# Chunk attention and a token-mixing MLP in one kernel: five units' exponentials taken from PSUM with a bias, and another order of steps and loads

## The chip, the cores and the metric

The kernel runs on one core of a Trainium2 chip. The metric is the device time of one execution in microseconds (us); a time without a unit is in us. Engines: TensorE (PE; its weight loads are PEld), VectorE (DVE), ScalarE (ACT), GpSimd (POOL) and SyncE (SP). POOL, SP and ACT can issue DMAs.

## The reference

Two stages, joined. Attention within chunks of 64 tokens (8 batches, 8 heads, 576 tokens, head size 64):

```python
scores = scale * np.matmul(q_c, k_c.transpose(0, 1, 2, 4, 3))
scores = scores - np.max(scores, axis=-1, keepdims=True)
attn = np.exp(scores)
attn = attn / (np.sum(attn, axis=-1, keepdims=True) + 1e-09)
out = np.matmul(attn, v_c)
```

Its output, with the heads side by side (x: 8 x 576 x 512), goes through the mixer, `relu((x wq)(x wk)^T x * scale) @ w_out`, with wq and wk of 512 x 64 and w_out of 512 x 512. The output is float32, 8 x 576 x 512; inside the kernel the operands of the matmuls are float16.

## The kernel before, in words

**Units.** The work is cut into 20 units, in the order of the list `pairs`. Of each batch, two units hold 256 tokens each (four chunks; "wide"), and the last 64 tokens of two batches make one unit of 128 tokens ("rest"). So units 0 and 1 are batch 0, unit 2 is the rest of batches 0 and 1, units 3 and 4 are batch 1, and so on; 2, 7, 12 and 17 are rests.

**Steps of a unit**, by the names that the code gives them:

- `tq`: PE transposes q, then k, into PSUM (L387, for a rest L372). `qkt`: ACT or DVE copy q's two halves into a block-diagonal tile `qbd` (64 partitions each; called qt below) and k into `kt` (L308, the helper `copy`).
- `S`: the scores into two PSUM banks (L407; a rest takes one). `mx`: DVE takes the maximum of every row (L420). `sub`: DVE subtracts it from the scores, out of PSUM into the SBUF tile `sh`; for wide units it also puts the tokens, which the loads interleave in twos, in their own order (L431, for a rest L427). `exp`: one ACTIVATE on ACT turns `sh` (128x1024 or 128x512) into the float16 tile `es` (L441).
- `E`: PE transposes `es` (L453); `et`: a copy out of PSUM. `V`: PE multiplies by v, with a column of ones that gives the sum (L484), in two halves for a wide unit. `den`, `rec`, `x`: DVE divides into `xs` (L498, L502, L512).
- `xT`, `xt`, `pj`, `wt`, `wkT`, `wkn`: the mixer's transposes, projections and copies (L536, L553, L569). `G`: the product of a batch (L607), copied as `g16`; `clr` clears a part of a `g16` tile beforehand. `mix`, `rm`: the product with g and the relu (L647; L667 on DVE, L669 on ACT). `out`: the last product (L696); `osb`: its copy out of PSUM, in two parts for a wide unit; then the store.

**The order.** Nothing is scheduled at run time. The steps are numbered as they are made, and the string `ORDER` lists the numbers with a letter for the engine: `p` PE, `a` ACT, `v` DVE, then PSUM banks; `206a` is exp of unit 7 on ACT, `207p4` its E in bank 4, `182` et of unit 6, `183` its first V. `i7.256` is a filler: a matmul of ones into bank 7 that nobody reads (L740); there are 52. `592s` sends the store of step 592. Each engine runs its own share of this list in its order, and waits at each instruction for what that instruction needs. The costs written beside the steps (`vec`, `act`, `quart`) served to make the order; they do nothing at run time.

**Loads.** The first unit's q and k come as float32 on SP's queue (L207) and are cast. All others go out on POOL's queue, cast to float16 on the way, in the order of `LOADS`: `q5` is q, then k of unit 5 (L215; L212 for a rest), `v3` its v in two DMAs (L229, L222), `wqk` and `wo` the weights (L233, L236). In the built program each DMA on this queue waits for the one eight before it. Loads are issued as early as `load_more` lets them: a v whose buffer is reused only after its user's V is in the list. Seven buffers serve q and k.

**Stores** go out on SP's queue. Until unit 4's v has been asked for they are kept in a list (`held`), and SP waits for that load with a tiny DMA (L268); the stores are at L271 and L275.

Of the kernel before, what the change touches and what calls it, by code (L numbers as in the profile page):

```python
# [29 lines left out]
class Banks:  # L30
# [8 lines left out]
HELD = 4  # L39
# [8 lines left out]
    "mx1": 2,  # L48
    "sh2": 2,
# [17 lines left out]
LOADS = "q1 v0 q2 v1 wqk v2 q3 q4 v3 q5 wo v4 q6 v5 q7 v6 q8 v7 q9 v8 q10 v9 q11 v10 q12 v11 q13 v12 q14 v13 q15 v14 q16 v15 q17 v16 q18 v17 q19 v18 v19"  # L67
# [5 lines left out]
0a 1v i7.256 i6.256 i5.256 i7.256 i6.256 i5.256 i7.256 i6.256 i5.256 i7.256 i6.256 i5.256 i7.256 i6.256 i5.256  # L73
i7.256 i6.256 i5.512 i7.256 i6.256 7p0 3a 2a 9a 8v i7.512 i6.512 i5.512 i7.512 i6.512 i5.512 i7.512 i6.256
i5.256 10p1 11a i7.256 26p5 28a 4a 27a i7.256 12p0 29p4 13v 30a 14v 15a i7.512 i6.512 i3.512 i7.512 i6.256 31p4
32v i7.512 i6.512 i3.512 i7.256 53p0 55v 33v i7.512 i6.256 16p1 54a 56a 17a 34a i7.512 i6.512 i3.512 i7.512
i6.256 18p0 22p6 i5.256 57p4 i3.512 35p5 36a 23v 19v 20v 58v 24v 59v 21v 37p2 41p4 38v 60a 39v 42v 25v 61p0
88p1 62a 63p6 89a 90a 45p0 40v 64v 43v 65v 44v 91p2 66v i3.256 47p1 92a 67p3 93p6 107p2 i5.512 110p4 109a 108a
68a 46a 48v 6v 94v 5v 95v 111v i3.256 69p5 49p3 70v 71p2 72v 112p4 113v 96a 50a 97p6 51p7 98a 52v 153p3 156p6
73p7.2 103p0 154a 155a 157a 75a 74a 114v 99p4 104v 105v 100v 101v 106v 102v 115a 158p2 76p6 159v 77a 78p0 116p4  # L80
126p5 79a 117v 160v 118p6 122p0 84p4 172p2 175p3 123v 124v 119v 125v 173v 174v 120v 85v 121v 161a 127a 162p5
176a 163a 177p2 168p4 164p0 128p6 129a 199p6 130p7 178v 165v 166v 179v 169v 167v 82p2 131v 170v 200a 202a 201a
180a 203p6 132p7 204v 83a 171v 181p3 234p2 133a 182a 134p7.0 183p4 237p3 236a 136a 235a 135v 205v 184v 185v
186v 238a 137p0 239p2 139p6 206a 138a 207p4 86p5 208a 140a 253p4 240v 241v 256p0 209p6 187p2 255a 254a 242a
143p1 191p4 192a 257v 188v 189v 190v 210v 211v 258p2 212v 259v 145p0 146a 260v 193p4 243p6 194a 244a 87a 87s
299p0 302p4 249p6 245p2 300a 301a 144v 213p5 214a 195p1 196a 261a 250v 251v 246v 303v 252v 247v 248v 215p0
304p4 80p6 149p2 216a 217p7 197p0 150a 198a 305v 218v 318p1 306v 219p0.7 321p2 221v 322v 220a 319a 320a 222p4
272p7 223v 224p2 273a 323p0 262p7 324v 225a 263a 307a 147p4 226p5 345p7 325v 268p0 264p2 148a 148s 81v 81s 269v
265v 270v 266v 271v 227v 267v 308p4 230p6 346a 348a 347a 326a 309a 231a 349p7 380p0 310p4 314p2 383p6 350v 351v
315v 311v 312v 316v 382a 381a 352a 274p1 327p7 328a 151p0 275a 384v 385p6 313v 317v 386v 276p1 353p2 277a 152a  # L90
152s 354a 387v 228p3 229v 229s 337p1 278p0 338a 279a 333p4 329p6 334v 330v 335v 331v 332v 336v 399p2 280p3.0
402p1 355p6 282v 356v 357v 358v 401a 281a 400a 388a 232p3 339p0 340a 283p4 284v 359p2 285p6 341p0 403a 360a
342a 233a 233s 286v 404p4 361p2 389p1 343p0 295p6 362a 363p2 344a 364a 390a 296a 405v 406v 445p3 365p2.0 448p1
366v 367a 447a 395p6 449v 289p0 141p2 370p4 293p1 142a 142s 407a 294a 290a 396v 397v 398v 446v 371v 450p2 451v
408p6 368p4 297p7 409a 369a 298a 298s 467p6 464p0 466a 465a 452v 468v 414p2 410p4 391p6 392v 411v 415v 393v
394v 412v 416v 413v 417v 291p1 376p0 469p6 470v 374p4 453a 454p5 375a 471v 455a 420p2 418p4 421a 419a 377a
491p5 456p2 460p6 287p4 472a 493v 494v 457v 492v 461v 462v 463v 495p5 458v 496v 497v 459v 422p0 378p6 423a 288a
288s 424p0 473p7 425a 529p4 426p0.5 474v 498a 379a 379s 530a 475p6 428v 479p2 427a 476v 480v 526p4 292a 292s
477v 481v 478v 545p0 527a 528a 482v 429p6 499p1 430v 431p2 531p4 500a 432a 485p1 532v 548p6 501p2 502v 439p7
547a 549a 546a 503v 504v 533v 483p6 440a 484a 486a 534a 505p0 550p2 372p7 441p4 487p1 535p6 373a 373s 442a 551v  # L100
506v 552v 437p7 507p0 536a 553a 537p2 488v 508v 541p4 538v 509p6 489p0 542v 539v 554p1 510a 543v 540v 544v 490a
555a 511p0.6 560p2 556p4 561v 557v 562v 558v 559v 563v 438a 438s 512a 513a 564p7 516p0 435p6 514p4 566p2 443p3
515v 565a 517a 567a 568p2 433p7 569a 444a 444s 570p2 436a 434a 434s 571v 522p4 572p6.5 524p7 525a 574v 573v
523v 523s 577p2 575p0 578a 518p7 520p6 576v 519a 521a 521s 589p0 581p7 583p6 585p2 579p3 590a 584a 584s 586a
586s 587p2 591p6 580v 592v 588v 582a 582s 592s 588s
# [4 lines left out]
def kernel(  # L110
# [10 lines left out]
    nc = tc.nc  # L121
# [74 lines left out]
    def load_qk(u):  # L196
        b, m = pairs[u]
        if m is None:
# [4 lines left out]
        for t, x in enumerate((q, k)):  # L203
            if u == 0:
                rows = x[b, :, 0 : 2 * P, :].rearrange("h (p r) d -> p h (r d)", r=R)
                wide_in.append(home("osb", [P, 2, DM], F32))
                nc.sync.dma_start(wide_in[t][:].rearrange("p i (h e) -> p (i h) e", e=R * D), rows)  # L207
                continue
            if m is None:
                for i in range(2):  # L210
                    rows = x[b + i, :, S - C : S, :].rearrange("h p d -> p h d")
                    nc.gpsimd.dma_start(qk[u][C * i : C * i + C, t], rows)  # L212
            else:
                rows = x[b, :, 2 * P * m : 2 * P * m + 2 * P, :].rearrange("h (p r) d -> p h (r d)", r=R)
                nc.gpsimd.dma_start(qk[u][:, t], rows)  # L215
# [26 lines left out]
    for e in LOADS.split():  # L242
        u = int(e[1:]) if e[1:].isdigit() else None
        rest = u is not None and pairs[u][1] is None
        if e == "wqk":
            landing("w", 1.7)
            loads.append((load_w, [], None))
        elif e == "wo":
            landing("wo", 3.3)
            loads.append((load_wo, [], None))  # L250
        elif e[0] == "q":
            for t in range(2):
                landing(("qk", u, t), 0.94 if rest else wide)
            loads.append((load_qk, [u], None))
        else:
            landing(("v", u), halves if rest else 2 * halves)
            loads.append((load_v, [u], next((w for w in heir_v if heir_v[w] == u), None)))


    made_v, held, opened = {None: 2}, [], []  # L260

    def load_more():
        while loads and made_v.get(loads[0][2], 0) == 2:
# [9 lines left out]
    def store(to, of):  # L273
        if opened:
            nc.sync.dma_start(to, of)  # L275
        else:
            held.append((to, of))
# [59 lines left out]
    def turns(u):  # L337
# [40 lines left out]
        for t in range(2):  # L378
            bk = Banks(1)

            def pe(t=t, bk=bk):
                tp = in_banks(bk, 512, F16)[:, 0].rearrange("p (j x r g) -> p j x r g", j=HP, x=4, r=R)
                for j in range(HP):
                    for r in range(R):
                        for o in range(2):
                            of = qk[u][:, t, 2 * j + o, r * D : r * D + D]
                            nc.tensor.transpose(tp[half(o), j, :, r, :], of, ident[:])  # L387

# [6 lines left out]
    def attention(u, made):  # L395
# [26 lines left out]

        def ev_sub(eng):
            sh = home(f"sh{ni}", [P, ng, C], F32)
# [14 lines left out]
        def ev_exp(eng):  # L439
            es = home(f"es{ni}", [P, ni * HP, 2 * C])  # L440
            nc.scalar.activation(  # L441
# [20 lines left out]
        n = add("sub", {"DVE": vec(ng * C)}, ev_sub, [n], reads=bs)  # L462
        n = add("exp", {"ACT": act(ng * C, True) + 0.018}, ev_exp, [n])
# [5 lines left out]
        for fours in ([0], [1]) if m is not None else ([0, 1],):  # L469
# [6 lines left out]
            def pe_v(fours=fours, xp=xp):  # L476
# [14 lines left out]
                made_v[u] = made_v.get(u, 0) + 1  # L491
                load_more()
# [190 lines left out]
    def outs(u, at_tok, deps):  # L683
# [4 lines left out]
        for i in range(ni):  # L688

            wide = DM // 2 if (b, m, i) == (B - 1, NPB - 1, 1) else DM  # L690
            for at in range(0, DM, wide):
# [17 lines left out]
                def send(i=i, s=s):  # L709
                    t0 = 0 if m is None else 2 * P * m  # L710
                    if m is None:
                        for c in range(2):
                            store(out[b + c, S - C : S, :], osb[0][half(c), i, :])
                    elif turned(u, 1):
                        store(out[b, t0 + i * P : t0 + i * P + P, s], osb[0][:, i, s])
                    else:
                        rows = out[b, t0 : t0 + 2 * P, :].rearrange("(x p) d -> p x d", p=C)
                        for c in range(2):
                            store(rows[:, 1:3] if c else rows[:, 0:4:3], osb[0][half(c)])
# [16 lines left out]
    for e in ORDER.split():  # L736
        what, eng, *at = re.split(r"([ipavs])", e, maxsplit=1)
# [5 lines left out]
        if eng == "s":  # L743
            n.send()
# [32 lines left out]
```

## Time and profile before

| | us |
|---|---|
| median of 3 runs | 138.56 |
| the runs | 138.06, 138.56, 140.58 |
| the profiled execution's own time | 138.08 |
| its span, first to last instruction | 136.3 |
| PE, DVE, ACT, POOL busy | 122.2, 109.6, 100.0, 74.3 |
| last matmul ends | 130.0 |
| E of unit 7 on PE begins | 47.94 |
| first store leaves, last load is issued | 55.70, 98.1 |

How to read it: busy time is an engine's own, fillers included; an instruction that waits is not busy. The profile's groups give busy time, the mean duration of one in ns, and the idle time of the engine just before the group with what ended it. Since the queues run in order, a start that follows the last one at once means that the queue was full, and a gap with a name behind it (`<-DVE sh`) means that the engine waited for that. A load's landing isn't in the list of instructions, but the wait of the load eight behind it ends with it.

### The profile page before, as it was taken

To read this page: it belongs to the slowest core of one execution; us is meant where nothing else is said; L and a number is where in the kernel's file an instruction comes from. 1 tells how busy PE (TensorE), PEld (TensorE's weight loads), DVE (VectorE), ACT (ScalarE), POOL (GpSimd) and SP (SyncE) were. 2 spreads that over 40 slices of the span, in tenths; PEclk is the share of its full clock that TensorE was granted. 3 is DMA by queue.
4 is the path that set the end of the run, shared out by engine and by line. 5 is a ranking of instruction groups with operands and counts; after the bars stand their busy time and mean duration, and the time that the engine had idled before them with its cause. 6 is when DMAs were issued, how large, how long until landed. Compare 5 with 4: busy or idle time off the path is not lost.

```text
span 136.3 us, 4971 instructions
## 1 busy us (share of the span) xinstructions
PE 122.2 (90%) x2124; PEld 82.8 (61%) x2124; DVE 109.6 (80%) x210; ACT 100.0 (73%) x175; POOL 74.3 (55%) x96
## 2 busy tenths in 40 slices
PE   6999978897859999999999999999999998999910
PEld 4566556575546667776676867566677766544500
DVE  5429898899899799999999999989989998535220
ACT  6186674789738997969996878795888998568500
POOL 7969998745789896469992642679410000000000
PEclk9999999999999999999999999999999999999997
DMA  3999999999999999999999999999999614628883
GB/s 83 273 169 155 131 171 170 182 190 175 156 156 170 172 176 170 166 236 153 173 207 292 175 279 185 241 207 220 200 164 300 227 37 121 154 64 206 280 248 124
DMA packets 86249, 25.08 MB, mean 184 GB/s; under 512 B 78932, under 2 KB 81748, under 8 KB 86228
## 3 DMA queue, kind: packets, MB, share of 16 engines
q0 software_dynamic: 78752, 14.29, 130.1%
q1 hardware_dynamic: 7476, 10.49, 25.3%
q8 instruction: 16, 0.26, 0.7%
q14 instruction: 5, 0.04, 0.1%
HBM read 29.62 MB, written 9.44 MB: 287 GB/s over the span
## 4 chain that ended last, share of the span: by engine, by line
PE 61%; DVE 20%; ACT 10%; issue 3%; DVEq 1%; ACTq 0%
PE ps L696 21%; PE ps L387 7%; DVE mx L420 6%; PE ps L740 5%; DVE sh L431 5%; PE ps L536 5%; PE ps L484 5%; PE ps L647 4%; PE ps L407 4%; PE ps L453 4%; PE ps L553 3%; ACT es L441 3%; PE ps L607 2%; DVE xs L512 2%; ACT rm L669 2%
## 5 line engine op out<-in xcount | busy, mean ns | idle before, releaser
L696 PE MATMUL ps<-wo,rm 128*128 128x512 f16 (+1 forms) x148 | 35.7, 374 | 0.0
L229 POOL DMA_DIRECT2D v_all<-in_v_dram x33 | 29.0, 896 | 11.5 <-DMA qk<-in_k_dram 4.4
L512 DVE TENSOR_TENSOR xs<-ps,rec 128x512 f16<-128x512 f32 x36 | 23.9, 684 | 0.4
L420 DVE TENSOR_REDUCE mx<-ps 128x16 f32<-128x1024 f32 (+1 forms) x20 | 22.2, 1110 | 1.5 <-PE ps L407 1.3
L441 ACT ACTIVATE es<-sh 128x1024 f16<-128x1024 f32 (+1 forms) x20 | 19.5, 975 | 2.7 <-DVE sh L431 2.5
L308 ACT COPY qbd<-ps 64x512 f32<-64x512 f32 (+1 forms) x33 | 18.1, 548 | 4.1 <-PE ps L387 2.4
L387 PE MATMUL ps<-ident,qk 128*64 128x128 f16 x512 | 19.6, 221 | 1.2 <-DMA qk<-in_k_dram 1.0
L696 PEld LDWEIGHTS <-rm 128*128 128x128 f16 x148 | 13.2, 98 | 12.2 <-issue 0.2
L308 ACT COPY osb<-ps 128x512 f32<-128x512 f32 (+1 forms) x28 | 15.8, 586 | 6.5 <-PE ps L696 6.4
L431 DVE TENSOR_TENSOR sh<-ps,mx 128x1024 f32<-128x1024 f32 x16 | 19.5, 1221 | 0.4
L387 PEld LDWEIGHTS <-qk 128*64 128x64 f16 x512 | 15.7, 109 | 4.7 <-issue 1.5
L215 POOL DMA_DIRECT2D qk<-in_k_dram x15 | 13.5, 902 | 3.4 <-DMA v_all<-in_v_dram 1.7
L215 POOL DMA_DIRECT2D qk<-in_q_dram x15 | 13.8, 918 | 1.8 <-DMA qk<-in_k_dram 1.4
L669 ACT ACTIVATE rm<-ps 128x1024 f16<-128x1024 f32 (+1 forms) x13 | 14.1, 1098 | 0.5 <-PE ps L569 0.3
L407 PEld LDWEIGHTS <-qbd 128*128 128x128 f16 x288 | 10.7, 98 | 4.5 <-DVE qbd L308 1.2
L740 PE MATMUL ps<-ones 128*128 128x256 f16 (+1 forms) x52 | 12.2, 372 | 1.2 <-DVE ones L157 1.2
L407 PE MATMUL ps<-kt,qbd 128*128 128x64 f16 x288 | 11.9, 193 | 1.1 <-DVE qbd L308 0.5
L308 ACT COPY xt<-ps 128x512 f32<-128x512 f32 (+1 forms) x18 | 9.6, 554 | 3.3 <-PE ps L536 3.0
L484 PE MATMUL ps<-v_all,et 64*64 64x65 f16 x576 | 9.8, 195 | 2.3 <-ACT et L308 0.7
L453 PE MATMUL ps<-ident,es 128*128 128x128 f16 x144 | 11.4, 220 | 0.2 <-DVE den L498 0.2
L308 ACT COPY et<-ps 128x512 f32<-128x512 f32 (+1 forms) x18 | 9.7, 541 | 2.0 <-PE ps L453 1.9
L536 PE MATMUL ps<-ident,xs 128*128 128x128 f16 x144 | 11.0, 220 | 0.1
(57 smaller groups left out, 172.5 us busy)
## 6 DMA issues: line engine op xcount, KB each, us to landing
out_dram<-osb SPq DMA_DIRECT2D x31, 256.0 KB, 5.2
v_all<-in_v_dram POOLq DMA_DIRECT2D x31, 128.0 KB, 7.7
qk<-in_q_dram POOLq DMA_DIRECT2D x15, 256.0 KB, 7.4
qk<-in_k_dram POOLq DMA_DIRECT2D x15, 256.0 KB, 8.0
out_dram<-osb SPq DMA_DIRECT2D x10, 128.0 KB, 2.8
v_all<-in_v_dram POOLq DMA_DIRECT2D x10, 64.0 KB, 6.3
osb<-in_q_dram SPq DMA_DIRECT2D x1, 512.0 KB, 4.2
osb<-in_k_dram SPq DMA_DIRECT2D x1, 512.0 KB, 5.5
```

Source lines behind the costliest of these rows:

```text
L215: nc.gpsimd.dma_start(qk[u][:, t], rows)
L229: nc.gpsimd.dma_start(v_all[on, slot[u] + i, :, 0:D], v[b, :, of, :].rearrange("h p d -> p h d"))
L308: (nc.vector.tensor_copy if eng == "DVE" else nc.scalar.copy)(to, of)
L387: nc.tensor.transpose(tp[half(o), j, :, r, :], of, ident[:])
L407: nc.tensor.matmul(sp[:, i, j, c ^ turned(u, i), :], lhsT=st["qb", u][:, j, x].rearrange("p o s -> p (o s)"), rhs=st["kt", u][:, j, x * C ...
L420: nc.vector.tensor_reduce(mx[:], scores(), axis=AX.X, op=ALU.max)
L431: nc.vector.tensor_tensor(out=sh[:].rearrange("p x (g r) -> p x r g", r=R), in0=in_banks(bs, 512).rearrange("p i (x r g) -> p (i x) r g", ...
L441: nc.scalar.activation(es[:].rearrange("p x s -> p (x s)"), st["sh", u][:].rearrange("p x s -> p (x s)"), AF.Exp, scale=scale_attn,)
L512: nc.vector.tensor_tensor(out=to, in0=xp()[:, :, :, 0:D], in1=by, op=ALU.mult)
L536: nc.tensor.transpose(tx[:, f, i, :], xs[u][:, i, 2 * f : 2 * f + 2, :], ident[:])
L696: nc.tensor.matmul(in_banks(bo, wide)[:, 0], lhsT=st["rm", key][:, f, at_tok + i * P : at_tok + i * P + P], rhs=wo[:, f, s], start=(f == 0 ...
L740: nc.tensor.matmul(ps[:, at[0], 0 : at[1]], lhsT=ones[:, 0:P], rhs=ones[:, 0 : at[1]], start=True, stop=True)
```

## The change

For units 0 to 4 (`DIRECT`) `sub` and `exp` are made in another way. `sub` becomes one DVE instruction on the 16 (rest: 8) maxima of a row, times minus the scale, into a small tile `nm`. `exp` becomes one ACTIVATE for each group of 64 scores that share a maximum, 16 in a wide unit and 8 in a rest, which reads the scores in PSUM and takes a column of `nm` as its bias; for wide units it writes with stride 2. The PSUM banks of the scores are now held until the last of these has read them.

The rest of the change: q and k of a unit can be loaded apart (`Q5`, `K5`), a q or k into a reused buffer is issued only after both transposes of the buffer's last user are in the list, and `LOADS` and `ORDER` are new. In the new order units 3 and 4 come before unit 2, there are 44 fillers in place of 52, several copies change between DVE and ACT (qt of units 1 and 3 and kt of unit 0 go to DVE in part or whole, xt of unit 1 to ACT), and the last store (`592t`) goes out on ACT's queue. The holding of stores is gone; each is issued where its step stands.

```diff
-HELD = 4
+DIRECT = 0, 1, 2, 3, 4
...
-LOADS = "q1 v0 q2 v1 wqk v2 q3 q4 v3 q5 wo v4 q6 v5 q7 v6 q8 v7 q9 v8 q10 ...
+LOADS = "Q1 K1 Q3 K3 Q4 v0 Q2 K2 K4 Q5 v1 K5 v2 wqk v3 Q6 v4 K6 Q7 v5 K7 wo v6 Q8 K8 Q9 K9 v7 Q10 K10 ...
...
+    made_of = {}
+    def load_more(key=None):
+        if key is not None:
+            made_of[key] = made_of.get(key, 0) + 1
+        while loads and (loads[0][2][1] is None or made_of.get(loads[0][2], 0) == 2):
             load, args, _ = loads.pop(0)
             load(*args)
-            if load is load_v and args == [HELD]:
-                nc.sync.dma_start(const.tile([1, 2], F16, name="held")[:], v_all[0:1, slot[HELD] + 1, H - 1, D - 2 : D])
-                opened.append(True)
-                for to, of in held:
-                    nc.sync.dma_start(to, of)
...
+        direct = u in DIRECT
         def ev_sub(eng):
+            if direct:
+                nm = home(f"nm{ni}", [P, ng], F32)
+                nc.vector.tensor_scalar(nm[:], st["mx", u][:], -scale_attn, None, op0=ALU.mult)
+                st["nm", u] = nm
+                return
...
         def ev_exp(eng):
             es = home(f"es{ni}", [P, ni * HP, 2 * C])
+            if direct:
+                for x in range(ng):
+                    to = es[:].rearrange("p x (c s) -> p (x c) s", c=2)[:, x]
+                    of = scores()[:, x]
+                    if m is not None:
+                        to = to.rearrange("p (g r) -> p r g", r=R)
+                        of = of.rearrange("p (r g) -> p r g", r=R)
+                    nc.scalar.activation(to, of, AF.Exp, bias=st["nm", u][:, x : x + 1], scale=scale_attn)
+                st["es", u] = es
+                return
...
-        if eng == "s":
-            n.send()
+        if eng in "st":
+            n.send(nc.sync if eng == "s" else nc.scalar)
```

ACT's share of the new order from exp of unit 0 to exp of unit 7: exp 0, kt 3, et 0, exp 1, qt 4, qt 2 (twice), qt 4, exp 3, kt 4, et 1, xt 0, exp 2, kt 5, et 2, exp 4, xt 1, et 3, xt 2, wt 0, et 4, exp 5, wt 2, wkn 2 (two casts into `wkr`), wkn 0, clr, qt 6, g16, xt 3, g16, xt 4, rm 0, exp 6, wt 3, kt 7, qt 7, wkn 3, et 6, osb, g16, exp 7. In front of exp 0 stand qt of unit 3 and kt of unit 1. On PE, between the first V of unit 6 (183) and E of unit 7 (207): the other V, one out, mix, tq of unit 8's q, xT of unit 5, tq of unit 8's k, mix.

More of the change, by code (lines that the diff above doesn't have):

```diff
@@ L48 @@
     "mx1": 2,
+    "nm2": 2,
+    "nm1": 1,
     "sh2": 2,
@@ L74 @@
[L74 to L78, printed above, removed]
@@ L194, with load_qk @@
     qk, wide, halves = {}, 0.0225 * 64, 0.0144 * 64
-    def load_qk(u):
+    def load_qk(u, ts=(0, 1)):
         b, m = pairs[u]
-        if m is None:
+        if u in qk:
+            pass
+        elif m is None:
             qk[u] = const.tile([P, 2, H, D], F16, name=f"qk{u}")
@@ L202, in load_qk @@
             qk[u] = const.tile(shape, F16, name="qk0") if u == 0 else home("qk", shape)
-        for t, x in enumerate((q, k)):
+        for t in ts:
+            x = (q, k)[t]
             if u == 0:
@@ L461, in attention @@
         n = add("mx", {"DVE": vec(ng * C)}, ev_mx, [n], reads=bs)
-        n = add("sub", {"DVE": vec(ng * C)}, ev_sub, [n], reads=bs)
-        n = add("exp", {"ACT": act(ng * C, True) + 0.018}, ev_exp, [n])
+        if direct:
+            n = add("sub", {"DVE": vec(ng)}, ev_sub, [n])
+            n = add("exp", {"ACT": ng * (act(C) + 0.017 * (ni - 1))}, ev_exp, [n], reads=bs)
+        else:
+            n = add("sub", {"DVE": vec(ng * C)}, ev_sub, [n], reads=bs)
+            n = add("exp", {"ACT": act(ng * C, True) + 0.018}, ev_exp, [n])
         n = add("E", {"PE": 4 * ni * 0.056}, pe_e, [n], form=FULL, takes=[be], size=4 * ni)
@@ L712, in send @@
                         for c in range(2):
-                            store(out[b + c, S - C : S, :], osb[0][half(c), i, :])
+                            by.dma_start(out[b + c, S - C : S, :], osb[0][half(c), i, :])
                     elif turned(u, 1):
-                        store(out[b, t0 + i * P : t0 + i * P + P, s], osb[0][:, i, s])
+                        by.dma_start(out[b, t0 + i * P : t0 + i * P + P, s], osb[0][:, i, s])
                     else:
@@ L718, in send @@
                         for c in range(2):
-                            store(rows[:, 1:3] if c else rows[:, 0:4:3], osb[0][half(c)])
+                            by.dma_start(rows[:, 1:3] if c else rows[:, 0:4:3], osb[0][half(c)])
                 n1 = add("out", {"PE": wide / 512 * 0.864}, pe_o, deps + [landed("wo")], form=FULL, takes=[bo], size=4)
```

91 lines of the change are left out of this document (44 added, 47 removed).

## The prediction

> **What bounds the kernel now.** I read the head of the page first, then the busy times by stage, the groups of instructions kept apart by shape, ScalarE's instructions in order of time, and the load queue beside TensorE at the place where they meet. The stages (columns PE, PEld, DVE, ACT, POOL busy, granted clock, DMA share, GB/s):
>
> ```profile
> PE 122.2 (90%) x2124; PEld 82.8 (61%) x2124; DVE 109.6 (80%) x210; ACT 100.0 (73%) x175; POOL 74.3 (55%) x96
> ```
> ```profile
> 12.00:48.00 36.00, 30.59 (x635) 21.61 (x632) 32.65 (x67) 26.17 (x44) 29.47 (x37) 1.00 1.98 167
> 48.00:70.00 22.00, 21.45 (x441) 15.57 (x440) 21.46 (x38) 19.63 (x35) 17.54 (x22) 1.00 1.97 179
> 70.00:130.00 60.00, 59.35 (x930) 38.51 (x928) 48.94 (x95) 46.90 (x87) 17.33 (x22) 1.00 1.29 200
> 130.00:136.30 6.30, 0.00 (x0) 0.00 (x0) 1.02 (x2) 0.00 (x0) 0.00 (x0) 0.89 0.59 175
> ```
>
> From 48 us to 130 us PE is busy 80.8 of 82 us: at most 1.2 us can be won there. The open stage is 12 to 48 us: DVE is busy 32.65 of 36 us and ACT only 26.17, and part of PE's 30.59 us is fillers (L740). So the kernel's end follows from when a given step is reached at about 48 us. I take E of unit 7 (step 207) as the mark: PE transposes its exponentials at 47.94 us. In front of it the two orders hold almost the same PE work (after: one S less at 0.47 us, one xT and one V more at 0.45 and 0.22), so after is 0.2 us of PE work ahead at this mark.
>
> The prices, by shape (busy us, mean ns):
>
> ```profile
> L431 DVE TENSOR_TENSOR sh<-ps,mx 128x1024 f32<-128x1024 f32 x16 | 19.5, 1221 | 0.4
> L441 ACT ACTIVATE es<-sh 128x1024 f16<-128x1024 f32 x16 | 17.0, 1061 | 2.7 <-DVE sh L431 2.5
> L498 DVE TENSOR_SCALAR den<-ps 128x8 f32<-128x8 f32 x36 | 5.1, 156 | 1.8 <-PE ps L484 1.4 <-ACT qbd L308 0.2
> L427 DVE TENSOR_TENSOR sh<-ps,mx 128x512 f32<-128x512 f32 x4 | 2.7, 687 | 0.1
> L441 ACT ACTIVATE es<-sh 128x512 f16<-128x512 f32 x4 | 2.5, 630 | 0.0
> L669 ACT ACTIVATE rm<-ps 128x512 f16<-128x512 f32 x4 | 2.4, 604 | 0.3 <-PE ps L569 0.3
> L308 ACT CAST wkr<-ps 64x64 f16<-64x64 f32 x4 | 0.8, 206 | 0.2
> ```
>
> ScalarE in order of time (start, duration):
>
> ```profile
> 45.93 0.58 ACT L308 COPY qbd<-ps 64x512 f32<-64x512 f32 x1
> 46.42 0.58 ACT L308 COPY kt<-ps 128x512 f32<-128x512 f32 x1
> 46.89 0.63 ACT L441 ACTIVATE es<-sh 128x512 f16<-128x512 f32 x1
> ...
> 82.24 0.44 ACT L308 CAST wkr<-ps 64x64 f16<-64x64 f32 x2
> ```
>
> A queued instruction starts 0.10 us before the last one ends (0.58 us long, 0.49 and 0.47 apart). The two 64-column casts do not overlap: 0.44 us for two of 0.206 is 0.234 from start to start.
>
> **The change, part by part.**
>
> *DVE loses* four wide subtractions and one narrow, and gains five multiplies of 16 or 8 numbers. By the den row: 4 x (1.221 - 0.156) + (0.687 - 0.156) = 4.8 us out of the busiest queue of the stage. It counts only if nothing else ends later.
>
> *ACT gains* 64 + 8 exponentials of 64 columns for four of 1.061 us and one of 0.630 us. No row has an ACTIVATE of 64 columns, or one with a bias per partition. Lower bound: the rm row's 604 ns less 448 columns at 0.833 ns (from 1061 and 630 ns: 0.84 a column) is 231 ns; less the overlap 0.10, with a bias that costs nothing, 0.13; plus the stride-2 write, (1317 - 1061) / 16 = 0.017 by the wide rm (L669, 1317 ns), about 0.15 us. Upper bound: an Exp from SBUF, 1061 - 960 x 0.833 = 0.261, no overlap, plus 0.017: 0.28. I take 0.25: the wkr pair's 0.234, the only row with 64 columns, plus 0.017; that says that the bias eats what the overlap gives. Then 64 x 0.25 + 8 x 0.23 = 17.8 us in place of 4.9.
>
> The Trainium skill (ScalarE: Activation LUTs, What ACT_TABLE_LOAD costs) states about 93 ns more for a bias pointer and an overlap of about 93 ns back to back; the trace's 0.10 agrees with the overlap, and no run here shows the pointer. By that page's 280 ns + 0.833 N, less 93, plus 0.017, one costs an estimated 0.257 us, and the sum below would come out 0.5 us later.
>
> *ACT's queue up to the mark.* Exp of unit 0 stands behind qt of unit 3 and kt of unit 1 on ACT. Their transposes stand behind unit 3's q, the third load; the first two landed at 8.4 and 9.9 us (POOL's waits end there), so 11.4 at the latest, and before's third, unit 0's v, was there by 10.8 (POOL issued the load eight behind it without a wait). I take 10.9; with a transpose and two copies (0.5 each) exp of unit 0 starts at about 12.4 us. From there to et of unit 6 (step 182) after's ACT queue holds, beside the 17.8: 14 copies of 512 columns at 0.49 (6.9), 3 half-partition copies at 0.58 (1.7), eight 256-column copies at 0.30, two g16 at 0.38, a clear at 0.41, a 128-column cast at 0.27 and the wkr pair at 0.44 (4.3), two wide exponentials at 0.97 (1.9) and one rm at 1.25: 16.1. About four times ACT needs PE's answer to its last step (E of unit 0, pj, E of unit 4, mix), 0.3 each: 1.2. So et of unit 6 ends at 12.4 + 17.8 + 16.1 + 1.2 = 47.5 us. PE then still has V of unit 6, one out, two mix halves, two tq and an xT before the mark: 0.45 + 0.86 + 0.86 + 1.0 + 0.45 = 3.6, so E of unit 7 at 51.1 against 47.94. Less the 0.2 of work done ahead: **3.0 us later**. The stall on DVE's subtraction is gone; what is late next is ACT's own queue, and V, xt and wt wait behind it.
>
> *Loads.* Each issue on POOL waits for the load eight before it. The bytes ahead of unit 8's k are the same in both orders. There the queue meets PE:
>
> ```profile
> 45.26 0.88 POOL L215 DMA_DIRECT2D qk<-in_k_dram  x1 [0.51 <-DMA qk<-in_k_dram]
> ...
> 45.56 0.64 PE L387 MATMUL ps<-ident,qk 128*64 128x128 f16 x16
> ```
>
> The first line's wait ended when unit 8's k landed (eight issues earlier); the second is its transpose, 0.3 us later. So the loads had no slack here, and after cannot reach this transpose before 45.3. It has 1.1 us more PE work in front of it there: that caps any early gain at about 1.1 us. Q and K apart, and units 3 and 4 loaded before the short unit 2, cost nothing while ACT is 3 us late; if ACT is not late, the loads are the next limit. Where buffers are reused (Q10 on), POOL waited for PE only twice for about 0.7 us; the new gate moves those waits, cost 0 to 0.7, taken as 0 since POOL idles 42 of the last 60 us of PE's stage.
>
> *Fillers:* eight fewer. They ran in gaps of PE; free, unless the clock drops (a rival).
>
> *Stores:* the held queue goes. Its marker DMA is 0.76 us of SP at 32.83, and the first store leaves only at 55.70: nothing, since outputs are not ready earlier. The last store moves to ACT's queue:
>
> ```profile
> 129.54 3.64 SPq L275 DMA_DIRECT2D out_dram<-osb x5
> ```
>
> SP issues at 0.73 us each and the last ends at 133.18, 2.1 us after DVE's last copy (131.05). With two of the issues on ACT up to 1.2 us could go, nothing if the 1.3 MB still to write is the limit (219 GB/s over 131 to 135). I take 0.5.
>
> **Sum:** +3.0 - 0.5 = +2.5 us on the profiled execution's own 138.08 (span 136.3, 1.8 around it): **140.6 us**. That execution lies 0.5 below the median of the runs shown (138.56), so this is 1.5% above the median.
>
> **Rivals.**
>
> (a) *The small exponentials overlap like copies and the bias is free* (0.15 each). ACT then ends 72 x 0.10 = 7.2 us sooner, but the loads cap the lead at 1.1 us at unit 8's k; with PE's idle 1.2 us of the later stage won as well, and the tail's 0.5: 138.1 - 2.8 = 135.3 us; with the cap alone 136.5. For it: the overlap is in every row of 128 partitions. Against: every instruction reads a new operand. It decides below about 0.21 us each, where ACT comes to the mark as early as before.
>
> (b) *The upper price*, 0.28: 72 x 0.03 = 2.2 more, 142.8 us. By the Trainium skill's figures (above) it would be 141.1, between this and my own.
>
> (c) *TensorE's clock falls in the stretched stage.* In the last stage the granted clock is 1.00 until 4.9 us after the last matmul and 0.50 from 135.0 on, so idling halves it. Twelve fillers of 256 columns at the start take 0.22 each, against 0.21 for a later one of 512. If it fell between the exponentials, five E, S and V rounds on ACT's path (0.45 each) would double: +2.3, 142.9 us. Against: no exponential group is longer than 4 us, and V, tq and S fall between.
>
> The Trainium skill (TensorE: Matmul & The Clock Gate, Part 1) gives about 3.4 us of idling for half rate; by it the gate is a closer call than by the 4.9 us of the trace, and (c) is what it would make of the time.
>
> **How the numbers follow.** A measurement of this kernel tells about 2% from no change, so 135.8 and 141.3 are the bounds. My price, between 0.22 and 0.26 each (138.4 to 141.3): 0.40. Rival (a), with any price under 0.22: 0.20, of which 0.12 pass 135.8. Rivals (b) and (c): 0.40, all beyond 141.3. So faster 0.12, within 2% 0.48, slower 0.40. The range 135.5 to 144.5 leaves out the best of (a) and (b) with (c) on top.
>
> **What would show it.** Right: 72 instructions of about 0.25 us on ACT; ACT busy over 90% from 13 to 47 us; exp of unit 0 taking 4 us; E of unit 7 near 51; DVE idle behind ACT. Wrong: starts 0.15 apart; E of unit 7 before 48; TensorE waiting for loads at unit 8 and after; a granted clock under 1.00 before 130 us; after 48 us, PE idle over 2 us.

## The result, and the profile after

The changed kernel takes 141.99 us (median of 4 runs, 141.22 to 142.66) against 138.39 (4 runs) for the kernel before: a ratio of 1.0254, 95% interval 1.0221 to 1.0287. It is 2.5% slower. The profiled execution of after took 142.66 us, span 140.6.

First the head of the page and the busy times by stage (columns as in the prediction):

```profile
PE 123.9 (88%) x2116; PEld 84.2 (60%) x2116; DVE 110.0 (78%) x219; ACT 107.4 (76%) x233; POOL 74.5 (53%) x96
```
```profile
12.00:48.00 36.00, 27.80 (x554) 20.92 (x548) 26.43 (x58) 32.07 (x108) 31.47 (x39) 0.91 2.04 170
48.00:70.00 22.00, 21.74 (x425) 15.74 (x425) 21.49 (x39) 19.08 (x34) 18.43 (x24) 1.00 2.06 174
```

Over the whole span hardly anything moved: ACT 7.4 us more, PE 1.7 more. The stage of 12 to 48 us shows the change: DVE fell from 32.65 to 26.43 us, ACT rose from 26.17 to 32.07, PE got less done (27.80 for 30.59) and its granted clock fell from 1.00 to 0.91. From 48 us on PE is as busy as before. The groups by shape (busy us, mean ns of one):

```profile
L452 ACT ACTIVATE es<-ps,nm 128x64 f16<-128x64 f32 x72 | 15.5, 393 | 0.0
L434 DVE TENSOR_TENSOR sh<-ps,mx 128x1024 f32<-128x1024 f32 x12 | 14.7, 1227 | 0.4
L424 DVE TENSOR_SCALAR nm<-mx 128x16 f32<-128x16 f32 x4 | 0.9, 228 | 0.1
```

ScalarE's exponentials of units 0, 1, 3, 2, 4 and 5 in order of time, with the two copies ahead of them (start, duration, [idle before]):

```profile
12.32 0.58 ACT L303 COPY qbd<-ps 64x512 f32<-64x512 f32 x1 [4.50 <-PE ps L382]
12.92 0.59 ACT L303 COPY kt<-ps 128x512 f32<-128x512 f32 x1
13.41 3.42 ACT L452 ACTIVATE es<-ps,nm 128x64 f16<-128x64 f32 x16
17.63 3.45 ACT L452 ACTIVATE es<-ps,nm 128x64 f16<-128x64 f32 x16
22.73 3.41 ACT L452 ACTIVATE es<-ps,nm 128x64 f16<-128x64 f32 x16
28.00 1.75 ACT L452 ACTIVATE es<-ps,nm 128x64 f16<-128x64 f32 x8
30.98 3.43 ACT L452 ACTIVATE es<-ps,nm 128x64 f16<-128x64 f32 x16
37.74 1.06 ACT L455 ACTIVATE es<-sh 128x1024 f16<-128x1024 f32 x1
```

Sixteen small ones take 3.42 us where one wide took 1.06. One is 0.393 long, so the starts are (3.42 - 0.393) / 15 = 0.202 us apart: short instructions overlap by almost half. The chain of waits shows what stood behind them (start, length, what):

```profile
17.77 3.32 ACT es L452 x16
21.09 0.04 issue
21.13 0.33 PE ps L502 x14
...
22.63 0.34 DVE kt L303
22.97 0.04 issue
23.01 0.58 PE ps L403 x8
23.60 1.84 PE ps L382 x16
```

One half of V of unit 0 (L502) needs a bank that holds unit 1's scores, and this is now held until the last of unit 1's exponentials has read them. Behind this V wait DVE's `den`, behind that kt of unit 2, and behind that S of unit 2 (L403). So PE does almost nothing from 20 to 23 us, and then its clock is down (seventh number: the granted clock):

```profile
20.00:23.00 3.00, 0.32 (x14) 0.30 (x14) 1.28 (x8) 2.96 (x12) 3.00 (x5) 0.83 2.13 168
23.00:26.00 3.00, 2.99 (x46) 2.66 (x46) 2.69 (x5) 3.00 (x17) 2.96 (x4) 0.50 2.33 154
26.00:30.00 4.00, 4.00 (x80) 3.22 (x78) 2.43 (x6) 3.42 (x12) 4.00 (x6) 0.65 2.07 164
```

At the mark, E of unit 7 on PE:

```profile
53.16 0.39 PE L467 MATMUL ps<-ident,es 128*128 128x128 f16 x4
```

That is 5.2 us after the 47.94 of before. From there to the end of the span after needs 87.4 us and before 88.4, so the span is 4.3 longer: 5.2 - 1.0, of which 0.6 are the last stores (5.7 us from the last matmul to the end, 6.3 before).

### The profile page after: what moved, and what is told of

It reads as the page before. It is cut to its first block, busy times and chain, and to the rows that moved or that the text cites. A ratio compares the mean times of both kernels' runs of the same rounds, so it can differ in the third digit from the quotient of the medians.

```text
span 140.6 us, 5012 instructions
## 1 busy us (share of the span) xinstructions
PE 123.9 (88%) x2116; PEld 84.2 (60%) x2116; DVE 110.0 (78%) x219; ACT 107.4 (76%) x233; POOL 74.5 (53%) x96
## 4 chain that ended last, share of the span: by engine, by line
PE 49%; ACT 18%; DVE 15%; DMA 8%; issue 3%; POOL 2%; SPq 0%; DVEq 0%; ACTq 0%; POOLq 0%
PE ps L713 15%; ACT es L452 7%; DMA qk<-in_q_dram 6%; PE ps L382 6%; PE ps L553 5%; PE ps L502 4%; PE ps L570 4%; DVE mx L416 4%; PE ps L664 4%; PE ps L403 4%; DVE sh L434 3%; PE ps L467 3%; PE ps L624 3%; DVE xs L529 3%; ACT kt L303 3%
## 5 line engine op out<-in xcount | busy, mean ns | idle before, releaser
L686 ACT ACTIVATE rm<-ps 128x1024 f16<-128x1024 f32 (+1 forms) x15 | 17.5, 1177 | 2.8 <-PE ps L664 2.6
L303 ACT COPY qbd<-ps 64x512 f32<-64x512 f32 (+1 forms) x22 | 11.7, 542 | 7.3 <-PE ps L382 7.0
L455 ACT ACTIVATE es<-sh 128x1024 f16<-128x1024 f32 (+1 forms) x15 | 14.6, 976 | 1.4 <-DVE sh L434 0.9
L452 ACT ACTIVATE es<-ps,nm 128x64 f16<-128x64 f32 x72 | 15.5, 393 | 0.0
L434 DVE TENSOR_TENSOR sh<-ps,mx 128x1024 f32<-128x1024 f32 x12 | 14.7, 1227 | 0.4
L303 ACT COPY osb<-ps 128x512 f32<-128x512 f32 (+1 forms) x23 | 13.1, 585 | 1.7 <-PE ps L713 1.6
L467 PE MATMUL ps<-ident,es 128*128 128x128 f16 x144 | 12.7, 225 | 1.3 <-ACT es L452 0.9
L403 PE MATMUL ps<-kt,qbd 128*128 128x64 f16 x288 | 12.3, 197 | 1.6 <-DVE kt L303 1.6
L403 PEld LDWEIGHTS <-qbd 128*128 128x128 f16 x288 | 11.1, 101 | 3.7 <-ACT qbd L303 1.5
L502 PE MATMUL ps<-v_all,et 64*64 64x65 f16 x576 | 10.3, 196 | 3.2 <-ACT es L452 1.3
L502 PEld LDWEIGHTS <-et 64*64 64x64 f16 x576 | 7.7, 107 | 8.5 <-issue 4.8
L303 DVE COPY qbd<-ps 64x512 f32<-64x512 f32 (+1 forms) x18 | 11.1, 624 | 2.1 <-ACT qbd L303 1.6
L467 PEld LDWEIGHTS <-es 128*128 128x128 f16 x144 | 9.6, 100 | 4.6 <-ACT es L452 1.6
```

The source lines that it names most:

```text
L303: (nc.vector.tensor_copy if eng == "DVE" else nc.scalar.copy)(to, of)
L403: nc.tensor.matmul(sp[:, i, j, c ^ turned(u, i), :], lhsT=st["qb", u][:, j, x].rearrange("p o s -> p (o s)"), rhs=st["kt", u][:, j, x * C ...
L434: nc.vector.tensor_tensor(out=sh[:].rearrange("p x (g r) -> p x r g", r=R), in0=in_banks(bs, 512).rearrange("p i (x r g) -> p (i x) r g", ...
L452: nc.scalar.activation(to, of, AF.Exp, bias=st["nm", u][:, x : x + 1], scale=scale_attn)
L467: nc.tensor.transpose(ep[:, x, :], es[:, x, :], ident[:])
L502: nc.tensor.matmul(to[half(k ^ i), i if ni == 2 else w, x, :], lhsT=et[half(k), i, h // 2, h % 2, :], rhs=v_all[half(k), slot[u] + i, h, 0:W],
```

## Experiments

The theories. **A**: the small exponentials fill ScalarE's queue, and its sum of work ends the stage. **B**: the new order and the new loads cost the time. **C**: the fall of TensorE's clock costs it. **D** came up on the way: only the exponentials of the first units count, because PE, DVE and the clock hang on them. All kernels, with three marks from the profiled execution of each (start in us), and the ratio to the kernel before:

| kernel | exp of unit 5 | E of unit 7 | span | median us | ratio, 95% interval |
|---|---|---|---|---|---|
| before | 35.13 | 47.94 | 136.3 | 138.39 | |
| after | 37.74 | 53.16 | 140.6 | 141.99 | 1.0254, 1.0221 to 1.0287 |
| e1 order alone | 34.28 | 49.68 | 137.2 | 139.31 | 1.0052, 1.0014 to 1.0089 |
| e2 small ones, old order | 49.12 | 61.85 | 150.2 | 151.47 | 1.0929, 1.0880 to 1.0977 |
| e3 no bias | 32.59 | 48.00 | 135.4 | 137.22 | 0.9883, 0.9829 to 0.9937 |
| e4 one wide, no bias | 31.36 | 46.77 | 134.3 | 136.39 | 0.9859, 0.9808 to 0.9911 |
| e5 one bias for the row | 32.82 | 48.23 | 135.7 | 137.71 | 0.9924, 0.9892 to 0.9957 |
| e6 V of unit 0 later | 35.80 | 51.21 | 138.6 | 140.85 | 1.0200, 1.0159 to 1.0240 |
| e7 k of unit 1 first | 36.63 | 52.04 | 139.6 | 141.20 | 1.0191, 1.0163 to 1.0220 |
| e8 one bias, old order | 39.23 | 51.53 | 139.9 | 141.75 | 1.0250, 1.0229 to 1.0271 |
| e9 e5, gap filled | 32.79 | 48.20 | 135.9 | 137.27 | 0.9914, 0.9883 to 0.9944 |
| e10 units 0, 1, 2 small | 37.11 | 52.52 | 140.0 | 142.33 | 1.0292, 1.0269 to 1.0315 |
| e11 e9, eight units | 32.82 | 49.17 | 136.8 | 138.87 | 1.0044, 1.0016 to 1.0073 |
| e12 units 3, 4 small | 34.57 | 49.98 | 137.6 | 138.90 | 1.0031, 1.0004 to 1.0059 |

Two columns settle where to look. From E of unit 7 to the end, all kernels in the new order need 87.4 to 87.7 us. From exp of unit 5 to E of unit 7 they need 15.40 to 15.42 us (e11, where unit 5 itself is changed, 16.35). So in the new order whatever an edit does is done before exp of unit 5. One thing moves the marks that no edit made: the landing of unit 3's q. The second of the two copies ahead of exp of unit 0 starts between 11.85 us (e5) and 12.92 (after), so marks of two executions can lie 1 us apart for that alone. Among the times, e1, e3, e4, e5, e9, e11 and e12 lie within 2% of before; of these, e3, e4, e5 and e9 have intervals that lie wholly under 1.

**e1, the order alone.**

```diff
-DIRECT = 0, 1, 2, 3, 4
+DIRECT = ()
```

> The changed kernel's order and loads, with subtraction and one wide exponential for all units as before. Theory A (the 72 small exponentials make ScalarE the queue that ends the stage): ScalarE gets back about 9.5 us of work, VectorE takes 4.8 us into a queue that idles 9.6 of the 36 us from 12 to 48; E of unit 7 moves from 53.2 us to 46 to 48 us and the time falls to 135 to 137 us. Theory B (the new order and the new loads cost it: unit 3's q in front of unit 0's exponentials, V of unit 0 behind unit 1's scores): E of unit 7 stays at 51 us or later, the time at 140 us or more. Theory C (TensorE's clock, granted 0.62 to 0.70 from 20 to 30 us): the granted clock is 1.00 throughout, and the part of the gain that C claims can't be told from A's here.

139.31 us: neither. The new order and loads by themselves are worth +0.5%; B does not explain 2.5%, and the gain that A hoped for isn't there either. DVE is busy 33.59 of 36 us from 12 to 48; that it bounds the stage with all the subtractions on it is argued from this row, not tested by itself. TensorE's clock fell here too (0.71 from 20 to 23, 0.72 from 23 to 26), where C expected 1.00.

**e2, the small exponentials alone**, in the old order and with the old loads:

```diff
+DIRECT = 0, 1, 2, 3, 4
...
-... 59v 21v 37p2 41p4 38v 60a 39v ...
+... 59v 60a 21v 37p2 41p4 38v 39v ...
```

(exp of unit 1, and in the same way that of unit 3, ahead of the V that takes its banks.)

> The kernel before, with the small exponentials for units 0 to 4 and nothing else: its own order, loads and stores (two exponentials stand a few places earlier in the list, ahead of a V that takes their banks; no engine's own order changes). Theory A: each unit's way from maximum to exponentials is 1.2 us longer (0.2 + 3.4 against 1.2 + 1.1 us), which VectorE's 4.8 us make good only in part: E of unit 7 moves from 47.9 to 50 to 53 us, the time to 140 to 143 us. Theory B: the exponentials fit into ScalarE's 9.8 idle us of the stage: E of unit 7 within 1 us of before, 137 to 139 us.

151.47 us, far more than expected. PE's waits from 12 to 48 us (total, times, longest):

```profile
PE ps L504 <- ACT es L458: 5.6, 3, 3.1
PE ps L760 <- ACT es L458: 2.6, 1, 2.6
PE ps L473 <- ACT es L458: 1.5, 5, 0.7
```

V (L504) and a filler (L760) wait for banks whose scores the exponentials have not yet read. PE runs in order, so everything behind them waits too: DVE falls to 16.89 us busy of 36. The clock was down as well (0.50 from 20 to 26 us), and no run tells its share of this loss. That order was made for banks that come free at the subtraction; the new one is what makes the small exponentials bearable at all (151.5 against 142.0).

**e3, no bias, and e4, one wide instruction without a bias.** Both leave the subtraction of the maximum out in units 0 to 4.

```diff
-nc.scalar.activation(to, of, AF.Exp, bias=st["nm", u][:, x : x + 1], scale=scale_attn)
+nc.scalar.activation(to, of, AF.Exp, scale=scale_attn)
```

> The changed kernel with the bias left out of the 72 small exponentials (the row's maximum is not subtracted in units 0 to 4; nm is still made). If the bias operand is what an instruction costs beyond an overlapped copy, the spacing falls from 0.205 us to 0.13 to 0.15 us, ScalarE gets back 4 to 5 us, and by theory A the time falls to 137 to 139 us. If the bias costs nothing, spacing and time stay (0.20 us, 142 us). By theory B the time stays whatever the spacing.

> The changed kernel with one wide exponential straight from PSUM for each of units 0 to 4 and no bias (the row's maximum is not subtracted there; nm is still made). ScalarE's work is that of the kernel before, about 1.3 us a unit with the strided write, and VectorE has no wide subtraction. Theory A: E of unit 7 at 44.5 to 46.5 us (unit 8's k, landed at 43.1, is the next limit), the time 133 to 136 us, a little under that of the order alone. Theory B: 140 us or more, since order and loads are the same.

Without the bias the 72 small ones are no longer a loss: 137.22 us, 4.8 less than after and 1.2% under before. Their group in e3:

```profile
L452 ACT ACTIVATE es<-ps 128x64 f16<-128x64 f32 x72 | 9.0, 332 | 0.0
```

Sixteen take 2.00 us, so they start (2.00 - 0.332) / 15 = 0.111 apart. The bias costs 0.202 - 0.111 = 0.091 us each. That decides between gain and loss here: the cost written beside these steps in the code is `ng * (act(C) + 0.017 * (ni - 1))` (L478), 0.120 us each by its `act`, about what they take without a bias. e4 (1.32 us for a wide one) takes 136.39 us, with E of unit 7 at 46.77: 0.4 and 0.3 beyond the ranges expected. That it is 0.8 under e3 is not shown to come from the wide instruction: the intervals overlap, and three of e4's runs have a mean clock of 0.988 or 0.989 and take 136.2 to 136.4 us, while its fourth, at 0.979, takes 137.55, more than any of e3's (136.0 to 137.5 at 0.978 to 0.991).

**e5, one bias for the whole row.** The largest of the row's 16 maxima shifts all its groups; one wide instruction.

```diff
-nm = home(f"nm{ni}", [P, ng], F32)
-nc.vector.tensor_scalar(nm[:], st["mx", u][:], -scale_attn, None, op0=ALU.mult)
+top = home(f"nm{ni}", [P, 1], F32)
+nc.vector.tensor_reduce(top[:], st["mx", u][:], axis=AX.X, op=ALU.max)
+nm = home(f"nm{ni}", [P, 1], F32)
+nc.vector.tensor_scalar(nm[:], top[:], -scale_attn, None, op0=ALU.mult)
...
+nc.scalar.activation(to, of, AF.Exp, bias=st["nm", u][:, 0:1], scale=scale_attn)
```

> The changed kernel, but one exponential for each of the units 0 to 4: ONE ScalarE instruction of 1024 (rest: 512) columns out of PSUM, with one bias for the whole row: minus the scale times the largest of its 16 (8) maxima, made by two small VectorE instructions. It shifts all groups of a row alike, so the quotient of the softmax is the same, but a group is no longer shifted by its own maximum. Theory A (the 72 small exponentials with a bias make ScalarE's queue end the stage): a wide one should take 1.32 us as in the run of one wide instruction, plus about 0.08 for the bias: 1.40, in place of 3.42; E of unit 7 at 46.8 to 48.0 us, 136.2 to 137.5 us, and so ahead of both kernels. Theory B (loads and order cost the time): E of unit 7 stays within 1.5 us of the changed kernel's, 140 us or more. Theory C (the clock): only what of the 0.62 to 0.83 clock between 20 and 30 us goes, 1 to 2 us.

137.71 us, 0.8% under before: ahead of both kernels, though by less than 2% of before; 0.2 above the range expected, as is E of unit 7 at 48.23.

```profile
L455 ACT ACTIVATE es<-ps,nm 128x1024 f16<-128x1024 f32 x4 | 5.6, 1408 | 0.6 <-DVE nm L426 0.6
```

1.408 against e4's 1.322: the bias costs 0.086 us here too, at 1024 columns much as at 64. Paid five times instead of 72 times, and in one wide instruction, it is no loss. B, which expected 140 or more, is out.

**e6, V of unit 0 later**, and **e7, k of unit 1 first.**

```diff
-... 22p0 53p4 109a 18p2 55a 19v 4v 54a 20v 23v 108a 24v 95v 56v 25v 96a 57p4 110p5 21v 153p0 58v
+... 22p0 53p4 109a 23v 24v 56v 95v 55a 4v 54a 108a 25v 96a 57p4 110p5 58v 18p2 19v 20v 21v 153p0
```
```diff
-... 88p0 29p4 90a 14v 27v 30a ...
+... 29p4 88p0 30a 14v 27v 90a ...
```

> The changed kernel with PE's first V of unit 0, which takes the banks of unit 1's scores, moved behind S of unit 2 and both transposes of unit 4, and VectorE's steps moved along (nm of unit 3 and kt of unit 2 ahead of den of unit 0); nothing else. Theory A (ScalarE's work alone ends the stage): ScalarE's queue has the same 31 us of work, so E of unit 7 moves by 0.8 us at most from 53.2 and the time stays between 141.0 and 142.3 us. Theory B (PE stands behind that bank): PE's gap of 20 to 23 us is filled, ScalarE's waits of some 3.5 us shrink by 1.5 to 3, E of unit 7 at 50 to 51.7, 139.0 to 140.5 us. Theory C (the clock): the gap is what halved the clock, so the granted clock of 23 to 30 us rises from 0.5 to 0.65 to 0.9 or more; it is right as a part of B if the clock rises and the time falls with it, and wrong if the clock rises and the time does not move.

> The changed kernel with the transposes of unit 1's k ahead of those of unit 3's q, on PE and on ScalarE (kt of unit 1 before qt of unit 3); nothing else. ScalarE then no longer waits for unit 3's q in front of kt of unit 1, but exp of unit 0 still stands behind qt of unit 3, so its own start can't move before that load. Theory A: what ScalarE does first changes nothing in its sum: E of unit 7 within 0.5 us of 53.2, 141.3 to 142.5 us. Theory B (the late start of S of unit 1 behind that load is part of the loss): S of unit 1 about 1 us earlier, E of unit 7 0.7 to 1.2 us earlier, 140.6 to 141.3 us.

Both are a little better than after by their ratios (about 0.5 and 0.6%; e6's interval overlaps after's, e7's ends where after's begins). E of unit 7 came 1.95 and 1.1 us sooner, but exp of unit 0 started at 12.37 and 13.13 in these executions and at 13.41 in after's, so 1.0 and 0.3 of that is when a load landed. In e6 PE was busy 1.58 of 3 us from 20 to 23 and the clock was still 0.58 from 23 to 26: S of unit 2 then waited 2.7 us for qt of unit 2, which stands behind unit 1's exponentials on ACT. The stall moved rather than went: counted from exp of unit 0, S of unit 2 starts 8.98 us later, against 9.60 in after, so the wait for the bank is worth 0.6 us there, and what is left of the delay stands in ACT's queue, which is busy 12.55 of the 12.59 us from 13.41 to 26 in after. B as a part (0.5% of the 2.5) can stand; C was not told apart.

**e8, one bias for the row in the old order** (the `DIRECT` and the moved steps of e2, the exponential of e5).

> The kernel before, with its own order and loads, and one ScalarE exponential out of PSUM with one bias for the row in units 0 to 4 (as in the run of one bias per row; two steps moved ahead of V of units 1 and 3 as in the run of the small exponentials alone). The banks of the scores are held until the exponential has read them, just as with the small ones. Theory A (the small ones' own length): ScalarE has 1.4 us a unit in place of 3.4, so the loss of the run of the small exponentials alone (151.5 us, E of unit 7 at 61.9) goes: E of unit 7 at 46.5 to 49.5, 137 to 140 us. Rival: this order needs the banks of the scores free at the subtraction, and holding them for any exponential is what cost 13 us there: E of unit 7 at 53 or later, 143 us or more.

141.75 us, between the two: of e2's 13 us, 9.7 go with the length of the small ones, and 3.4 stay. They fit the rival: PE still waits 3.8 us for exponentials that hold banks (V 2.7, a filler 0.8, a transpose 0.3), though the clock, 0.87 and 0.85 from 30 to 42 us, has a share that isn't told apart. Here, taking scores straight from PSUM needs an order made for it, even if the exponential is short: the same exponential gains in the new order (e5).

**e10, units 0, 1 and 2 small, and e12, units 3 and 4 small**, each with wide exponentials and subtractions elsewhere.

```diff
-DIRECT = 0, 1, 2, 3, 4
+DIRECT = 0, 1, 2
```
```diff
-DIRECT = 0, 1, 2, 3, 4
+DIRECT = 3, 4
```

> The changed kernel with the small exponentials in units 0, 1 and 2 only; units 3 and 4 are subtracted by VectorE and take one wide exponential again, in the changed order. Theory A (ScalarE's queue, 2.4 us more for each wide unit with small ones): two units less take 4.7 us off ScalarE and put 2.1 on VectorE, so E of unit 7 falls from 53.2 to between 49.5 and 51.3, 0.8 to 1.8% above the kernel before. Theory B (order and the wait of V of unit 0 behind unit 1's exponentials): both are as before, and happen ahead of these two units' exponentials but for one, so E of unit 7 stays at 52.3 or later, 2% or more above the kernel before.

> The changed kernel with the small exponentials in units 3 and 4 only; units 0, 1 and 2 are subtracted by VectorE and take one wide exponential, in the changed order: the complement of the run with units 0, 1 and 2 small, which kept the whole loss (E of unit 7 at 52.5, exp of unit 5 at 37.1) although ScalarE had 4.7 us less to do. Theory A (ScalarE's sum counts, whichever units it is): two wide units of small ones put 4.7 us on ScalarE over the run of the order alone (E of unit 7 at 49.7), so about half of the loss should be there: E of unit 7 at 50.8 to 52, 140.3 to 141.2 us. Theory D (the first two count: units 0 and 1 fill ScalarE from 13.4 to 20.1 us, V of unit 0 waits for their banks, PE idles, its clock halves from 23 us on and PE itself then ends the stage up to 30 us; units 3 and 4 run beside that): E of unit 7 at 49.2 to 50.5, 138.8 to 139.9 us, and no wait of V for exponentials over 0.5 us before 21 us.

142.33 and 138.90 us. The marks, first of e10, then of e12:

```profile
52.52 0.39 PE L467 MATMUL ps<-ident,es 128*128 128x128 f16 x4
```
```profile
49.98 0.39 PE L467 MATMUL ps<-ident,es 128*128 128x128 f16 x4
```

Theory A, by which the sum over the stage counts, falls: 4.7 us less work for ScalarE (e10) brings nothing in the time, and 4.7 us more than in e1 (e12) costs 0.3 at the mark and nothing in the time. Neither run moves ScalarE's work alone, since the subtractions go to or from DVE; in e10 that of unit 3 stands ahead of kt of unit 2, and S of unit 2 waits 2.6 us for this kt, 1.6 in after.

Against e1's 49.68, units 0, 1 and 2 cost 2.8 us, units 3 and 4 cost 0.3, all five 3.5. But unit 3's q landed 0.8 to 1.0 us sooner in e1 and e10 than in e12 and after: counted from the second copy ahead of exp of unit 0, E of unit 7 comes 37.8 us later in e1, 40.6 in e10, 37.3 in e12 and 40.2 in after. So counted, all five cost 2.5, units 0, 1 and 2 alone no less, and units 3 and 4 nothing.

In e10 V of unit 0 waits 1.3 us for unit 1's exponentials and PE's clock is 0.50 from 23 to 26, as in after; in e12 V waits for none of them, and the clock, though it falls, is back sooner (0.64 from 20 to 23, 0.79 from 23 to 26, then 1.00; 0.62 from 26 to 30 in e10). How these become the loss is read from S and E of unit 2 on PE, first in after, then in e12:

```profile
23.01 0.58 PE L403 MATMUL ps<-kt,qbd 128*128 128x64 f16 x8 [1.56 <-DVE kt L303]
...
30.12 0.40 PE L467 MATMUL ps<-ident,es 128*128 128x128 f16 x4
```
```profile
21.00 0.59 PE L403 MATMUL ps<-kt,qbd 128*128 128x64 f16 x8 [1.96 <-ACT qbd L303]
...
26.97 0.40 PE L467 MATMUL ps<-ident,es 128*128 128x128 f16 x4
```

S of unit 2 starts 2.0 us later in after (0.2 of it the landing of q). From S to E of unit 2, after needs 7.1 us, with PE busy all the time, and e12 6.0; e4, whose clock stays at 1.00, needs 4.7 (20.14 to 24.83). From there to the mark both need 23.0. So of the 3.2 us between after and e12 about 1.1 pass while PE runs at the lower clock. D holds: the first units' exponentials, back to back on ACT and with PE's and DVE's next steps behind them, are the loss, and the clock is a part of how they cost it. No run separates unit 2's from those of units 0 and 1; E of unit 2 follows the transposes in front of it without a wait in after and in e10.

**e9, e5 with the gap filled, and e11, that with units 5, 6 and 7 as well.**

```diff
-... i4.512 22p0 53p4 109a 18p2 55a 19v ... 95v 56v 25v
+... i4.512 22p0 i2.512 i3.512 53p4 109a 18p2 55a 56v 19v ... 95v 25v
```

> The run of one bias per row with two edits of order around 17 to 20 us: kt of unit 2 on VectorE ahead of den of unit 0, so that S of unit 2 can start about 1 us sooner, and two fillers (512 columns, in the banks of unit 1's scores) ahead of the transposes of unit 2, where PE waits for a load. Theory C (the clock): the runs of one bias per row fell into two groups, 136.5 to 136.6 us at a mean clock of 0.988 and 137.3 to 138.3 at 0.977 to 0.983, and the profiled one shows 0.68 to 0.73 between 20 and 26 us behind an idle PE (0.99 us busy of 3 from 17 to 20). With the gap filled the clock should stay at 1.00 there and nearly all runs be of the first group: 136.0 to 136.7 us. Rival (the two groups have another cause, or the gap does not set the clock): the clock dips all the same or the time stays, median 137.3 to 138.0.

> The run of one bias per row with the gap filled, with units 5, 6 and 7 made in the same way as well (eight units). VectorE was 5.9 of 6 us busy from 42 to 54 us; it loses 2 x 0.9 + 0.4 us there, and ScalarE gains 2 x 0.35. If VectorE still ends the stage: E of unit 7 0.8 to 2 us earlier than in that run, 135 to 136 us. If the loads or PE end it: within 0.3 us of that run. If holding the banks of the scores costs more here, where the order counts on their being free at the subtraction: later by 0.5 us or more.

e9: 137.27 us, E of unit 7 at 48.20; exp of unit 0 started 0.7 us later than in e5's profile (13.04 against 12.33), so that counted from there the mark comes 0.7 us sooner. PE's two windows:

```profile
17.00:20.00 3.00, 1.53 (x42) 1.05 (x42) 1.76 (x4) 1.96 (x5) 3.00 (x4) 1.00 1.97 174
20.00:23.00 3.00, 2.81 (x45) 2.56 (x46) 2.85 (x12) 2.37 (x4) 3.00 (x5) 0.60 2.12 168
```

PE was busier ahead of 20 us (1.53 us, 0.99 in e5), and the clock still fell. The runs fall into the same two groups: mean clock 0.987 to 0.990 with 136.5 to 136.9 us, 0.977 to 0.978 with 137.6 to 138.0. So a lower mean clock goes with 1.0 us, run by run, in one and the same kernel, but filling this gap in part does not prevent it. e11 is 1.2% slower than e9: with unit 5's banks held until its exponential, V waits 1.1 us for it, and E of unit 7 is 1.0 later. The third of its expected cases came.

## Why the prediction was right and wrong

The time (140.6 forecast, 141.99 measured) lies within its range. The likeliest case, within 2%, was not the one that came: it is 2.5% slower. The sum was made for the profiled execution, which took 142.66, 2.1 over. It came as near as that by luck: two errors, the price and ACT's waits, nearly cancelled. With the price as measured and nothing else altered it gives 140.6 - 2.9 = 137.7 us, no loss at all; the prediction itself says that below about 0.21 us each ACT comes to the mark as early as before.

- **The mark and what follows it: right.** E of unit 7 stands for the end in every kernel. The later stage gave 0.3 us, the last stores 0.6 (0.5 forecast).
- **The price: too high.** 0.25 was taken, 0.202 measured, between the bounds of 0.15 and 0.28. By the bars above, each less the 0.10 us by which the next instruction overlaps it, 72 cost 4 x 3.3 + 1.65 = 14.9 us and not 17.8. The premise that "the bias eats what the overlap gives" was wrong: the overlap is twice what the longer rows show, and the bias costs 0.09. The Trainium skill (ScalarE: Activation LUTs, What ACT_TABLE_LOAD costs) gave 93 ns for the pointer; the 91 and 86 ns here agree, while its overlap of 93 ns does not: here it is 0.393 - 0.202 = 0.19.
- **Start: 1.0 us too early** (12.4 forecast, 13.41). Unit 3's q landed at 11.6, not 10.9. It differs by up to 1 us between the executions of the new order.
- **ACT's waits: the step that failed.** "About four times ACT needs PE's answer to its last step", 1.2 us in all. From 13.41 to the end of et of unit 6 at 48.47 are 35.1 us; less 14.9 and the 16.1 of other work, 4.1 remain (3.6 by ACT's row of busy times, 31.48 of 35.06 us). All but 0.04 of these 3.6 us come after 26 us: up to there ACT's queue is full, as the prediction has it, and then it waits for a PE that is late and slow. The scores' banks are held longer, and the prediction never followed who takes them next: V of unit 0, with DVE behind it, and S of unit 2 behind that (0.6 us, e6). Nor did its sum let PE's clock fall (about 1 us, by S and E of unit 2). So ScalarE's sum over the stage is not what ends it (e10, e12).
- **From et of unit 6 to the mark: 4.7 us, not 3.6.** The forecast counted PE's work alone; the 15.4 us from exp of unit 5 are the same in ten kernels, in after with DVE busy 5.73 of 6 us from 42 to 48 and 5.90 from 48 to 54. That DVE sets them is argued: e11, which takes work from DVE there, came out later for another reason.
- **Loads at unit 8: right.** They had no part.
- **Rival (a):** a free bias is what e3 tries. It gave 137.2 us against the 135.3 to 136.5 worked out; the sign was right, and in the changed kernel the bias is not free. **Rival (b)** is out by the price.
- **Rival (c), the clock: dismissed too lightly.** "V, tq and S fall between": V did not, it waited for the exponentials. The clock was 0.50 to 0.65 from 23 to 30 us. After's own runs lie at 141.2 to 141.5 and at 142.5 to 142.7, mean clocks 0.979 to 0.991 and 0.954 to 0.967; so the deeper fall is worth about 1.2 us in the runs that have it, and without it after is still 2.1% slower (141.35 against 138.39). This is read from runs of one kernel, not steered by an experiment. What sets it off stays open: e6 and e9 made the idle stretch shorter and the clock fell all the same, while e4's profile, with PE busy 1.02 of 3 us from 17 to 20, has none.
- **Its signs.** Of those named for being right, DVE idle behind ACT came, ACT was busy 90% from 13 to 47 us, and exp of unit 0 took 3.4 us, not 4, with E of unit 7 2 us past 51. Of those for being wrong, the granted clock under 1.00 before 130 us came.

## What to carry to other kernels

Splitting one wide ScalarE instruction into many with a bias each costs 0.2 us apiece here, 0.09 of it the bias; one bias per row, where the mathematics allows a common shift, was 0.8% faster than before (argued, not tried: a group whose own maximum lies far below the row's loses precision). When a reader of PSUM gets slower, ask first who takes its banks next and what stands behind that on the same queue, before summing its engine's work. A planner's price for a new kind of instruction (0.120 here) is worth one measurement ahead of the search.

## What was not expected of the hardware

- A per-partition bias adds 0.09 us to an ACTIVATE at 64 columns and at 1024 alike.
- ACTIVATEs of 64 columns out of PSUM overlap by 0.19 us (with a bias) to 0.22 (without: 0.332 long, 0.111 apart), where copies of 512 columns overlap by 0.10.
- The mean granted clock of one kernel's executions falls into two groups, whose times lie 1.0 us (e9) to 1.2 us (after) apart. In the profiled ones it fell without a long idle stretch: in e9 PE was busy for half of the 3 us ahead of it. The Trainium skill (TensorE: Matmul & The Clock Gate, Part 1) has a free-running window of about 3.4 us judge how busy PE was; that two runs of one kernel differ agrees with it, but idle time of its length was not needed here.
